# Moving two gate tiles out of the first V buffer, and cutting the last transfers of a cached decode step

## The chip, the cores and the metric

The kernel runs on one core of one Trainium2 chip. The metric is the device time of one execution in microseconds. One execution was also taken by the hardware profiler; its span runs from the first to the last instruction, and its own time is a little longer than that span.

## What is computed

One decode step for two tokens (B = 2, D = 512) with 32 heads of 128 and a cache of 8192 positions per head, all in float32.

```
xn = layernorm(x)
q  = (xn @ wq) as 64 pairs (b, h) of 128
p  = softmax(q . k_cache * 128**-0.5)        # 8192 positions per pair
s  = (p . v_cache) as (2, 4096) @ wo
y  = layernorm(xn)
g  = silu(gelu(y @ w1 + b1) @ w2 + b2)       # F = 1376
out = x + s * g
```

The K cache and the V cache hold 268 MB each. wq and wo are 8.4 MB each, w1 and w2 2.8 MB each. Every byte is read once.

## The kernel before

**Tiles and loop.** The 64 pairs of batch and head are taken two at a time (U = 2): each of N = 32 steps handles 128 partitions by 128 positions by 128 channels, a tile of 8.4 MB for K and one for V. Three buffers of that size exist: `KBUF[0]` and `KBUF[1]` (`big[0]`, `big[1]`) for K, and `VB` (`big[2]`) for V. In step n, DVE multiplies the K tile by the query in place (line 277), reduces it to the scores `SC` (line 278), and takes the row maxima `MX`; PE transposes these, DVE reduces them to `nm`, and PE broadcasts them; ACT turns the scores into the weights `PZ` (line 295) and sums them. PE then multiplies `PZ` with the V tile into the PSUM tile `po` (`weighted`, line 395), ACT copies that to `o4`, and PE folds it into `OT`.

**Order of the work.** There is no planner: `Program.op` writes each instruction to its engine's own queue, with semaphore waits, in the order of the source. Nearly all loads are issued by SP, in source order: the weights, K0 (line 189), K1 (line 266, after the query projection has read wq out of `big[1]`), V0 (line 289), and then in step n the pair K(n+2), V(n+1) (lines 299 and 300). K(n+2) waits for the scores of step n (`k_done`), since it overwrites that buffer; V(n+1) waits for the V product of step n. In step N - 2 the buffer `KBUF[0]` takes the last V tile instead of a K tile (line 302, semaphore `d_v31`), and wo is loaded into `VB` in four pieces along its rows (`WO_CUTS`, lines 303 to 306) once the V product of step N - 2 has read `VB`.

**What the first V buffer holds before V0.** The setup puts small tiles into `big[2]` with `boot` (lines 112 to 122): w1, w2, the layernorm tiles, b2, `q_nat`, `sel`, `z`, `th`, `q_all`. `z` and `th` belong to the gate: ACT copies the second MLP product `pgate` to `z` and takes its tanh into `th` (lines 262 and 263); DVE combines both into `gate` (line 284). That DVE instruction stands in step 0 after the scores of K0. So SP may issue V0 only when `gate` is there:

```
            wait("SP", t["gate"], t["sel"], t["qnat"], pe("pgate"))
            op("SP", "dma_start", VB, vf[0], sig="d_v")
```

**PSUM.** Eight banks are shared between setup and loop. The 64 query rows are spread over partitions by PE into `PB[0]` and `PB[1]` in turn and copied to `Q` by ACT, four steps' worth at a time (line 254). `PB[0]` is bank 0, which later is `po`; `pqa` (the gathered queries) is bank 4, which later is `acc`, the accumulator of the wo product. Both accumulators are zeroed by DVE behind those uses (lines 258 and 259), ahead of the first K multiply in DVE's queue.

**The end.** After the last V product the numerators `OT` and the sums `RS` are rearranged (`Z`, `ZL`, `OA`) and divided (`on`, line 317). The wo product (lines 423 to 428) runs over 32 rows; all rows of a piece wait for that piece's semaphore. DVE multiplies `acc` by the gate, adds x, and two small stores write the result.

Of the kernel before, what the change touches and what calls it, by code (L numbers as in the profile page):

```python
# [13 lines left out]
class Program:  # L14
# [24 lines left out]
    def wait(self, eng, *tokens):  # L39
        for name, v in self.need(eng, tokens):  # L40
            self.engines[eng].wait_ge(self.sem(name), v)
# [5 lines left out]
    def op(self, eng, method, *args, waits=(), sig=None, quiet=False, **kwargs):  # L47
        need = self.need(eng, waits)
        for name, v in need[:-1]:
            self.engines[eng].wait_ge(self.sem(name), v)  # L50
        ins = getattr(self.engines[eng], method)(*args, **kwargs)  # L51
        for name, v in need[-1:]:
            ins._wait_ge(self.sem(name), v)
        if quiet:
            return None
        name = sig or "own_" + eng
        by = 16 if method == "dma_start" else 1
        ins.then_inc(self.sem(name), by)
        self.counts[name] += by
        return name, self.counts[name]  # L60


def decode_kernel(nc, x, kc, vc, wq, wo, w1, b1, w2, b2, out):
    P = 128
# [4 lines left out]
    U = 2  # L69
    HP = P // U  # L70
    KP = S // HP
    HH = H // U
    N = B * HH
# [5 lines left out]
    JW = 512 // DH  # L79
# [4 lines left out]
    OC = DH // PH  # L84
    BH = B * H
    NPB = 512 // DH
    WO_CUTS = (0, 24, 29, 31, 32)

    pr = Program(nc)
    op, wait, take = pr.op, pr.wait, pr.take  # L90

    def sb(shape, name):
        return nc.alloc_sbuf_tensor(name, list(shape), F32).ap()
# [5 lines left out]
    vf = vc.rearrange("b h s d -> (b h s d)").rearrange("(n p j d) -> n p j d", p=P, j=KP, d=DH)  # L99
# [3 lines left out]
    KBUF, VB = rows[:2], rows[2]  # L103
    used = [0]

    def boot(p, n):
        a = used[0]
        used[0] += n
        assert used[0] <= KP * DH
        return big[2][:p, a:a + n]  # L110
# [6 lines left out]
    b2_sb = boot(1, D)  # L117
    q_nat = boot(P, NG // QT * 512).rearrange("p (n c) -> p n c", c=512)
    sel = boot(P, P)
    z = boot(P, P)  # L120
    th = boot(P, P)
    q_all = boot(BH, DH)
    wq_sb = big[1].rearrange("p (c n) -> p c n", n=H * DH)
    wo_sb = big[2].rearrange("p (c n) -> p c n", n=D)
# [1 line left out]
    Q = sb([P, N, DH], "Q")  # L126
# [4 lines left out]
    mod = sb([P, R], "mod")  # L131
# [3 lines left out]
    x4 = sb([P, P], "x4")  # L135
    gate = sb([P, P], "gate")
    res = sb([P, P], "res")
    xnT = sb([P, ND, B], "xnT")
    yT = sb([P, ND, B], "yT")
    hT = sb([P, NF + 1, B], "hT")  # L140
# [13 lines left out]
    on = sb([P, B, OC], "on")  # L154

    bank = [ps([P, 512], f"bank{i}") for i in range(8)]
    po = bank[0]
# [3 lines left out]
    acc = bank[4][:, :P]  # L161
    OA = bank[5][:, :B * (OC + 1)].rearrange("p (b c) -> p b c", c=OC + 1)
    pgate = bank[6][:, :P]
    ph = bank[7][:, :(NF + 1) * B]
    PQ = [bank[1], bank[2]]
    pxn, py = bank[3][:, :ND * B], bank[5][:, :ND * B]
    pqa = bank[4][:, :P]
    PB = [bank[0], bank[7]]

    PE_EVENTS = ["xnT", "yT", "ph", "pq", "pqa"] + [f"pb{g}" for g in range(N // NPB)] + ["pgate"]  # L170

    def pe(name):
        return "pe_setup", PE_EVENTS.index(name) + 1

    def pe_n(name, n):
        return name, n + 1

    t = {}
# [12 lines left out]
    for b in range(B):  # L191
        t["x4"] = op("ACT", "dma_start", x4[b::R, :], x[b, 0].rearrange("(j n) -> j n", n=P), sig="d_x4",
                     waits=[t["x4m"]])
# [11 lines left out]
    for s in range(U):  # L205
        t["half"] = op("DVE", "memset", half[HP * s:HP * (s + 1), PH * s:PH * (s + 1)], 1.0, waits=[a])
    a = op("DVE", "memset", sel, 0.0)
    for k in (1, 2, 6):
        t["mem"] = op("DVE", "memset", bank[k], 0.0)
    by_row = ident.rearrange("p (j r) -> p r j", r=R)  # L210
    t["mod"] = op("DVE", "tensor_reduce", out=mod, in_=by_row, axis=AX.X, op=ALU.add, waits=[t["ident"]])
# [1 line left out]
                  op=ALU.add)  # L213
    t["sel"] = op("DVE", "tensor_copy",
                  sel[:, HP:].rearrange("p (b j r) -> p b j r", b=B, r=HG)[:, :, :QT, 0], by_row[:, :B, :],
                  waits=[a])
# [23 lines left out]
    c = op("DVE", "tensor_mul", gu, gh, gh, waits=[a])  # L240
    c = op("DVE", "tensor_scalar", gu, gu, GELU_A, 1.0, op0=ALU.mult, op1=ALU.add, waits=[c])
    c = op("DVE", "tensor_mul", gu, gu, gh, waits=[c])
    c = op("ACT", "activation", gu, gu, AF.Tanh, scale=GELU_C, waits=[c])
    c = op("DVE", "scalar_tensor_tensor", gu, gu, 1.0, gh, op0=ALU.add, op1=ALU.mult, waits=[c])
    c = op("DVE", "tensor_scalar_mul", hT, gu, 0.5, waits=[c])
# [7 lines left out]
    for g in range(N // NPB):  # L253
        t[f"Q{g}"] = op("ACT", "copy", Q[:, g * NPB:(g + 1) * NPB, :],
                        PB[g % 2].rearrange("p (n d) -> p n d", d=DH), waits=[pe(f"pb{g}")])
        for n in range(g * NPB, (g + 1) * NPB):
            Qt[n] = t[f"Q{g}"]
    t["po0"] = op("DVE", "memset", po, 0.0, waits=[t[f"Q{N // NPB - 2}"]])
    t["acc0"] = op("DVE", "memset", acc, 0.0, waits=[t["qall"]])


    t["z"] = op("ACT", "copy", z, pgate, waits=[pe("pgate")])
# [7 lines left out]
    for n in range(N):  # L270
        k = KBUF[n % U]
        if n:

            op("ACT", "copy", o4, po, sig="s_o4", waits=[pe_n("p_v", n - 1)])
            t["OT"] = op("ACT", "copy", OT[:, U * (n - 1):U * n], pt[:, :U], waits=[pe_n("p_t", n - 1)])
        qb = Q[:, n, :].unsqueeze(1).to_broadcast([P, KP, DH])
        a = op("DVE", "tensor_tensor", out=k, in0=k, in1=qb, op=ALU.mult, waits=[k_land[n], Qt[n]])
        a = op("DVE", "tensor_reduce", out=SC[n % 2], in_=k, axis=AX.X, op=ALU.add, waits=[a], sig="v_k")
        k_done = a
        op("DVE", "tensor_reduce", out=MX, in_=SC[n % 2], axis=AX.X, op=ALU.max, waits=[a], sig="v_mx")  # L280
        op("DVE", "tensor_reduce", out=nm, in_=pm[:1, :P].rearrange("o (s r) -> o s r", s=U), axis=AX.X,
           op=ALU.max, negate=True, waits=[pe_n("p_m", n)], sig="v_nm")
        if n == 0:
            a = op("DVE", "scalar_tensor_tensor", gate, th, 1.0, z, op0=ALU.add, op1=ALU.mult,
                   waits=[t["th"], t["pool"]])
            t["gate"] = a

            wait("SP", t["gate"], t["sel"], t["qnat"], pe("pgate"))
            op("SP", "dma_start", VB, vf[0], sig="d_v")
            t["v_last"] = None  # L290
        a = op("ACT", "copy", bias, pn[:, :1], waits=[pe_n("p_n", n)])
        sc = SC[n % 2].rearrange("p (t j) -> p t j", j=JW)
        for s in range(U):
            r = slice(HP * s, HP * (s + 1))
            op("ACT", "activation", PZ[r, :, s, :], sc[r], AF.Exp, bias=bias[r], scale=SCALE,
               accum_out=RS[r, n:n + 1], waits=[a, t["pool"]], sig="s_pz")
        m = n + 2
        if m < N:
            k_land[m] = op("SP", "dma_start", KBUF[m % U], kf[m], sig=f"d_k{m % U}", waits=[k_done])
            op("SP", "dma_start", VB, vf[m - 1], sig="d_v", waits=[pe_n("p_v", m - 2)])  # L300
        elif m == N:
            op("SP", "dma_start", KBUF[m % U], vf[N - 1], sig="d_v31", waits=[k_done])
            wait("SP", pe_n("p_v", N - 2))
            wo_v = wo.rearrange("(p c) n -> p c n", p=P)
            for i, (c0, c1) in enumerate(zip(WO_CUTS, WO_CUTS[1:])):
                op("SP", "dma_start", wo_sb[:, c0:c1], wo_v[:, c0:c1], sig=f"d_wo{i}")
# [10 lines left out]
    t["on"] = op("DVE", "tensor_tensor", out=on, in0=OA[:, :, :OC], in1=rl.unsqueeze(2).to_broadcast([P, B, OC]),  # L317
                 op=ALU.mult, waits=[a])
    a = op("DVE", "scalar_tensor_tensor", res, acc, 0.5, gate, op0=ALU.mult, op1=ALU.mult,
           waits=[pe_n("p_acc", 0), t["gate"], t["acc0"]])  # L320
    t["res"] = op("DVE", "tensor_add", res, res, x4, waits=[a, t["x4"]])
    for b, eng in enumerate(("SP", "ACT")):
        t[f"o{b}"] = op(eng, "dma_start", out[b, 0].rearrange("(j n) -> j n", n=P), res[b::R, :], sig=f"d_o{b}",
                        waits=[t["res"]])
# [22 lines left out]
    for f in range(NF + 1):  # L347
        for c in range(ND):
            w = w1_sb[:, c, f:NF * P:NF] if f < NF else w1_sb[:, c, F - P:]
            last = f == NF and c == ND - 1  # L350
            mm(ph[:, f * B:(f + 1) * B], w, yT[:, c, :], start=c == 0, stop=c == ND - 1,
               waits=[t["yT"], ("d_w1", 16)], sig="ph" if last else None)
    for n in range(NG // QT):
        for c in range(ND):
            for j in range(QT):
                g = n * QT + j
                last = n == NG // QT - 1 and c == ND - 1 and j == QT - 1
                mm(PQ[n][R * j:R * j + B, :], xnT[:, c, :], wq_sb[:, c, g * 512:(g + 1) * 512], start=c == 0,
                   stop=c == ND - 1, waits=[t["xnT"], t["mem"], ("d_wq", 16)], sig="pq" if last else None)
    for n in range(NG // QT):  # L360
        for hh in range(HG):
            a = HP - (n * QT * HG + hh)
            last = n == NG // QT - 1 and hh == HG - 1
            mm(pqa[:BH, :], sel[:, a:a + BH], q_nat[:, n, hh * DH:(hh + 1) * DH], start=n + hh == 0, stop=last,
               waits=[t["sel"], t["qnat"]], sig="pqa" if last else None)
# [13 lines left out]
    for f in range(NF + 1):  # L379
        for j in range(QT):  # L380
            mm(pgate[R * j:R * j + B, :], hT[:, f, :], w2_sb[:, f, j * P:(j + 1) * P], start=f == 0, stop=False,
               waits=[t["hT"], t["w2"], t["mem"]])
    for j in range(QT):
        mm(pgate[R * j:R * j + B, :], ones[:1, :B], b2_sb[:, j * P:(j + 1) * P], start=False, stop=True,
           waits=[t["b"]], sig="pgate" if j == QT - 1 else None)
# [8 lines left out]

    def weighted(v, last=False):
        take("PE", "s_pz", U)
        if last:
            nc.tensor.wait_ge(pr.sem("d_v31"), 16)
        else:
            take("PE", "d_v", 16)  # L400
        for i in range(NT):
            j = i % QT
            mm(po[R * j:R * j + U * JW, :], PZ[:, i].rearrange("p s j -> p (s j)"),
               v[:, i * JW:(i + 1) * JW, :].rearrange("p j d -> p (j d)"), start=i < QT, stop=i + QT >= NT,
               sig="p_v" if i == NT - 1 else None)
        take("PE", "s_o4")
        for i in range(JW):
            mm(pt[:, :U], o4[:, i * DH:(i + 1) * DH], mod[:, i:U * JW:JW], start=i == 0, stop=i == JW - 1,
               sig="p_t" if i == JW - 1 else None)

    wait("PE", t["po0"], t["pool"], t["mod"])
    softmax()
    with nc.tensor.Fori(0, N - 1):
        weighted(VB)
        softmax()
    weighted(KBUF[0], last=True)

    for b in range(B):
        h = slice(b * H, (b + 1) * H)
        mm(OA[:, b, :OC], Z[:, h].rearrange("p h r -> p (h r)"), mod, waits=[t["Z"]])  # L420
        m = slice(b * HH, (b + 1) * HH)
        mm(OA[:, b, OC:], ZL[:, m].rearrange("p n r -> p (n r)"), ones[:, :1], sig="p_oa" if b == B - 1 else None)
    for i, (c0, c1) in enumerate(zip(WO_CUTS, WO_CUTS[1:])):
        for c in range(c0, c1):
            for j in range(QT):
                last = c == OC - 1 and j == QT - 1
                mm(acc[R * j:R * j + B, :], on[:, :, c], wo_sb[:, c, j * P:(j + 1) * P], start=c == 0,
                   stop=c == OC - 1, waits=[t["on"], t["acc0"], (f"d_wo{i}", 16)], sig="p_acc" if last else None)


_INS = ["A_x", "A_k_cache", "A_v_cache", "A_wq", "A_wo", "B_w1", "B_b1", "B_w2", "B_b2"]
# [23 lines left out]
```

## Time and profile before

| | |
|---|---|
| runs | 1323.99, 1325.63, 1325.75 us, median 1325.63 us |
| profiled execution, its own time | 1324.34 us |
| its span | 1322.9 us |
| DVE busy | 1129.2 us (85%) |
| PE busy | 396.9 us (30%) |
| ACT busy | 70.5 us (5%) |
| read from memory | 559.37 MB, mean 423 GB/s over the span |
| granted TensorE clock, mean | 0.637 |

How to read the profile: times are microseconds from the start of the span. The engines are PE (matmul), PEld (weight load), DVE, ACT, POOL and SP; a trailing q means the queue that issues transfers. A group of instructions is given as line, engine, operation, what it writes and reads by the program's names, shapes, count, busy time and mean duration in ns, and the idle time before it with what ended it. As nearly all instructions are recorded by one helper, they carry that helper's line, L51 (L41 to L50 for its waits), and the names of the tiles tell them apart. A matmul in float32 shows as two records. "GB/s" and "PEclk" give the bytes moved and the granted TensorE clock in equal slices of the span.

### The profile page before, as it was taken

The numbers are of one execution on the slowest core, as the hardware profiler recorded it, in microseconds if no ns is written. First come the engines' busy times: TensorE is split into PE (matmuls) and PEld (weight loads), VectorE is DVE, ScalarE is ACT, GpSimd is POOL, SyncE is SP. The second block draws the span as 40 slices with busy tenths as digits, with TensorE's granted clock in tenths as the row PEclk, the third lists the DMA queues.
The fourth block names the chain that finished last, engine by engine and source line by source line (L and its number), as shares of the span: only waits on it lengthen the run. The fifth ranks groups of instructions, "written<-read, shape, count | busy, mean of one in ns | idle before, by whom it ended". The sixth has DMA issues, their size and how long they took to land. (4 is left out here: it accounts for less than half of the span.)

```text
span 1322.9 us, 7003 instructions
## 1 busy us (share of the span) xinstructions
PE 396.9 (30%) x3128; PEld 144.7 (11%) x3128; DVE 1129.2 (85%) x166; ACT 70.5 (5%) x244; POOL 1.1 (0%) x8
## 2 busy tenths in 40 slices
PE   6603211333231233322123332212333221233336
PEld 6300000000000001000000000000000000000003
DVE  1298988888988888898888889888889988888991
ACT  1100000000000000000000000000000000000000
POOL 0000000000000000000000000000000000000000
PEclk9956656666655666665566666556666655666657
DMA  9939999999999999999999999999999999999997
GB/s 413 427 159 444 432 424 442 430 429 442 430 428 442 430 428 442 434 424 442 438 420 442 438 420 442 440 418 440 442 418 440 442 418 440 442 418 440 442 418 318
DMA packets 10704, 559.51 MB, mean 423 GB/s; under 512 B 1459, under 2 KB 1475, under 8 KB 1862
## 3 DMA queue, kind: packets, MB, share of 16 engines
q1 hardware_dynamic: 10666, 559.36, 97.9%
q8 instruction: 6, 0.10, 0.0%
q14 instruction: 4, 0.03, 0.0%
q10 hardware_dynamic: 28, 0.01, 0.0%
HBM read 559.37 MB, written 0.00 MB: 423 GB/s over the span
## 5 line engine op out<-in xcount | busy, mean ns | idle before, releaser
L51 DVE TENSOR_TENSOR big<-big,Q 128x16384 f32<-128x16384 f32 x32 | 551.2, 17224 | 96.1 <-DMA big<-in_A_k_cache_dram 96.1
L51 DVE TENSOR_REDUCE sc<-big 128x128 f32<-128x16384 f32 x32 | 551.0, 17220 | 1.1
L51 PE MATMUL bank<-big,PZ 128*8 128x512 f32 x2048 | 287.9, 725 | 689.2 <-PEq L45 686.7
L51 PEld LDWEIGHTS bank<-big,PZ 128*8 128x8 f32 x2048 | 59.7, 102 | 890.4 <-issue 887.8
L51 ACT COPY o<-bank 128x512 f32<-128x512 f32 x32 | 18.7, 585 | 939.8 <-PE bank L51 939.8
L51 PE MATMUL bank<-ident,MX 128*1 128x128 f32 x32 | 11.9, 372 | 172.1 <-PEq L45 172.1
L51 PE MATMUL bank<-mod,o 128*128 128x2 f32 x256 | 32.8, 250 | 25.7 <-PEq L45 25.7
L51 PEld LDWEIGHTS bank<-mod,o 128*128 128x128 f32 x256 | 31.0, 191 | 54.4 <-issue 54.4
L51 ACT ACTIVATE PZ<-sc,bias 64x128 f32<-64x128 f32 x64 | 25.5, 399 | 1.9
L51 DVE TENSOR_REDUCE nm<-bank 1x2 f32<-1x128 f32 x32 | 8.9, 279 | 17.8 <-PE bank L51 17.8
L51 DVE MEMSET bank<- 128x512 f32 (+1 forms) x5 | 2.1, 421 | 25.3 <-ACT Q L51 25.1
L51 PEld LDWEIGHTS bank<-ident,MX 128*1 128x1 f32 x32 | 2.5, 79 | 174.1 <-issue 174.1
L51 PE MATMUL bank<-yT,big 128*128 128x2 f32 x88 | 19.9, 364 | 1.9 <-DMA big<-in_B_w_dram 1.9
L51 PEld LDWEIGHTS bank<-yT,big 128*128 128x128 f32 x88 | 19.9, 322 | 2.0 <-DMA big<-in_B_w_dram 2.0
L51 DVE TENSOR_TENSOR gh<-bank,b_sb 128x22 f32<-128x22 f32 x1 | 0.2, 181 | 22.7 <-PE bank L51 22.7
L51 PE MATMUL bank<-nm,srow 1*64 1x1 f32 x128 | 12.0, 243 | 14.8 <-PEq L45 14.8
L51 ACT COPY bias<-bank 128x1 f32<-128x1 f32 x32 | 5.1, 160 | 205.3 <-PE bank L51 205.3
L51 PEld LDWEIGHTS bank<-nm,srow 1*64 1x64 f32 x128 | 10.2, 200 | 24.2 <-issue 24.2
L51 DVE TENSOR_TENSOR Z<-blk,OT 128x256 f32<-128x256 f32 x1 | 0.4, 425 | 14.0 <-ACT OT L51 14.0
L51 ACT ACTIVATION_READ_ACCUMULATOR PZ<-sc,bias 64x1 f32 x64 | 11.8, 185 | 0.0
L51 PE MATMUL bank<-big,xnT 128*2 128x512 f32 x64 | 9.1, 732 | 6.9 <-DMA big<-in_A_wq_dram 6.9
L51 DVE TENSOR_REDUCE MX<-sc 128x1 f32<-128x128 f32 x32 | 9.1, 286 | 1.1
(64 smaller groups left out, 69.4 us busy)
## 6 DMA issues: line engine op xcount, KB each, us to landing
big<-in_A_wo_dram SPq DMA_DIRECT2D x1, 6144.0 KB, 23.7
big<-in_B_w_dram SPq DMA_DIRECT2D x1, 2752.0 KB, 9.4
big<-in_B_w_dram SPq DMA_DIRECT2D x1, 2560.0 KB, 14.9
big<-in_A_wo_dram SPq DMA_DIRECT2D x1, 1280.0 KB, 26.4
big<-in_A_k_cache_dram SPq DMA_DIRECT2D x32, 42.9
big<-in_A_v_cache_dram SPq DMA_DIRECT2D x32, 29.5
big<-in_A_wo_dram SPq DMA_DIRECT2D x1, 512.0 KB, 27.2
big<-in_B_w_dram SPq DMA_DIRECT2D x1, 256.0 KB, 15.3
```

The source lines that it names most:

```text
L51: ins = getattr(self.engines[eng], method)(*args, **kwargs)
```

## The change

- `z` and `th` get tiles of their own in place of parts of `big[2]`. SP's wait ahead of V0 drops `gate`.
- `PB[0]` moves from bank 0 to bank 3 and `pqa` from bank 4 to bank 5. The two later memsets of `po` and `acc` go; banks 4 and 0 are zeroed with banks 1, 2 and 6 at the start, whole.
- The last V tile is loaded in two halves with a semaphore each, and PE waits for a half at a time.
- wo is loaded in seven pieces of 10, 8, 6, 4, 2, 1 and 1 rows in place of 24, 5, 2 and 1.

```diff
-    WO_CUTS = (0, 24, 29, 31, 32)
+    WO_CUTS = (0, 10, 18, 24, 28, 30, 31, 32)
+    V_CUTS = (0, KP // 2, KP)
...
-    z = boot(P, P)
-    th = boot(P, P)
...
+    z = sb([P, P], "z")
+    th = sb([P, P], "th")
...
-    pqa = bank[4][:, :P]
-    PB = [bank[0], bank[7]]
+    pqa = bank[5][:, :P]
+    PB = [bank[3], bank[7]]
...
-    for k in (1, 2, 6):
+    for k in (1, 2, 6, 4, 0):
         t["mem"] = op("DVE", "memset", bank[k], 0.0)
...
-    t["po0"] = op("DVE", "memset", po, 0.0, waits=[t[f"Q{N // NPB - 2}"]])
-    t["acc0"] = op("DVE", "memset", acc, 0.0, waits=[t["qall"]])
...
-            wait("SP", t["gate"], t["sel"], t["qnat"], pe("pgate"))
+            wait("SP", t["sel"], t["qnat"], pe("pgate"))
             op("SP", "dma_start", VB, vf[0], sig="d_v")
-            t["v_last"] = None
...
-            op("SP", "dma_start", KBUF[m % U], vf[N - 1], sig="d_v31", waits=[k_done])
+            for i, (c0, c1) in enumerate(zip(V_CUTS, V_CUTS[1:])):
+                op("SP", "dma_start", KBUF[m % U][:, c0:c1], vf[N - 1][:, c0:c1], sig=f"d_v31{i}", waits=[k_done])
...
-           waits=[pe_n("p_acc", 0), t["gate"], t["acc0"]])
+           waits=[pe_n("p_acc", 0), t["gate"]])
...
-        if last:
-            nc.tensor.wait_ge(pr.sem("d_v31"), 16)
-        else:
+        if not last:
             take("PE", "d_v", 16)
         for i in range(NT):
+            if last and i * JW in V_CUTS:
+                nc.tensor.wait_ge(pr.sem(f"d_v31{V_CUTS.index(i * JW)}"), 16)
...
-    wait("PE", t["po0"], t["pool"], t["mod"])
+    wait("PE", t["mem"], t["pool"], t["mod"])
...
-                   stop=c == OC - 1, waits=[t["on"], t["acc0"], (f"d_wo{i}", 16)], sig="p_acc" if last else None)
+                   stop=c == OC - 1, waits=[t["on"], t["mem"], (f"d_wo{i}", 16)], sig="p_acc" if last else None)
```

## The prediction, made before the result was known

> **What bounds the kernel now.** I read the page first: its slices, queues, groups and transfer list.
>
> ```profile
> GB/s 413 427 159 444 432 424 442 430 429 442 430 428 442 430 428 442 434 424 442 438 420 442 438 420 442 440 418 440 442 418 440 442 418 440 442 418 440 442 418 318
> q1 hardware_dynamic: 10666, 559.36, 97.9%
> L51 DVE TENSOR_TENSOR big<-big,Q 128x16384 f32<-128x16384 f32 x32 | 551.2, 17224 | 96.1 <-DMA big<-in_A_k_cache_dram 96.1
> L51 DVE TENSOR_REDUCE sc<-big 128x128 f32<-128x16384 f32 x32 | 551.0, 17220 | 1.1
> ...
> big<-in_A_wo_dram SPq DMA_DIRECT2D x1, 6144.0 KB, 23.7
> big<-in_A_wo_dram SPq DMA_DIRECT2D x1, 1280.0 KB, 26.4
> big<-in_A_k_cache_dram SPq DMA_DIRECT2D x32, 42.9
> big<-in_A_v_cache_dram SPq DMA_DIRECT2D x32, 29.5
> big<-in_A_wo_dram SPq DMA_DIRECT2D x1, 512.0 KB, 27.2
> big<-in_A_wo_dram SPq DMA_DIRECT2D x1, 256.0 KB, 27.3
> ```
>
> DVE is busiest, but in the loop it waits for K: 96.1 us of idle time before its multiplies ends with a K transfer. The stream from memory runs at 413 to 444 GB/s in every slice but two: the third (159) and the last (318). A K tile takes 42.9 us from issue to landing, more than twice its own transfer (below), so other transfers always lie ahead of it. So the stream sets the pace, and the time is its bytes, plus its pauses, plus what follows its last byte. The change has to be priced on these.
>
> The cadence comes from the timeline of DVE late in the loop, the pause from the windows around the third slice.
>
> ```profile
> 1219.67 17.23 DVE L51 TENSOR_TENSOR big<-big,Q 128x16384 f32<-128x16384 f32 x1 [3.07 <-DMA big<-in_A_k_cache_dram]
> 1258.38 17.23 DVE L51 TENSOR_TENSOR big<-big,Q 128x16384 f32<-128x16384 f32 x1 [3.08 <-DMA big<-in_A_k_cache_dram]
> ...
> 73.00:74.00 1.00, 0.00 (x0) 0.00 (x0) 1.00 (x1) 0.00 (x0) 0.00 (x0) 0.50 0.31 131
> 74.00:93.00 19.00, 0.37 (x1) 0.08 (x1) 18.38 (x4) 0.00 (x0) 0.00 (x0) 0.50 0.00 0
> 93.00:94.00 1.00, 0.38 (x4) 0.32 (x4) 1.00 (x3) 0.21 (x2) 0.00 (x0) 0.50 0.00 0
> 94.00:1296.00 1202.00, 333.90 (x2387) 100.33 (x2387) 1084.53 (x124) 59.39 (x221) 0.00 (x0) 0.62 1.00 433
> ```
>
> One step of K and V takes 1258.38 - 1219.67 = 38.7 us, so one tile 19.35 us. The last column is GB/s: 131 in 73 to 74 is 0.13 MB, 0.3 us at 433 GB/s; then nothing until 94.0. The pause is 73.3 to 94.0, **20.7 us**. From 94 to 1296 there is no other (share 1.00).
>
> What ended it is in the timelines of SP, DVE, PE and the waits of SP's queue:
>
> ```profile
> SPq L51 <- DVE gate L51: 31.9, 1, 31.9
> ...
> 93.36 0.33 SPq L51 DMA_DIRECT2D big<-in_A_v_cache_dram  x1
> 93.74 0.42 SPq L51 DMA_DIRECT2D big<-in_A_k_cache_dram  x1
> 124.69 0.33 SPq L51 DMA_DIRECT2D big<-in_A_v_cache_dram  x1
> 127.75 0.33 SPq L51 DMA_DIRECT2D big<-in_A_k_cache_dram  x1
> ...
> 61.00 0.40 PE L51 MATMUL bank<-big,ones 1*2 1x128 f32 x8
> ...
> 56.98 0.63 DVE L51 MEMSET bank<- 128x512 f32 x2 [25.07 <-ACT Q L51]
> 57.52 17.21 DVE L51 TENSOR_TENSOR big<-big,Q 128x16384 f32<-128x16384 f32 x1
> 74.76 17.22 DVE L51 TENSOR_REDUCE sc<-big 128x128 f32<-128x16384 f32 x1
> 92.01 0.29 DVE L51 TENSOR_REDUCE MX<-sc 128x1 f32<-128x128 f32 x1
> ```
>
> SP sat 31.9 us on `gate`, a small DVE instruction queued behind the 34.4 us of K0's multiply and reduce. `pgate`, the other thing V0 needs, is done at 61.40.
>
> **V0 without the gate.** SP now issues V0 at about 61.5, while K1 is still moving until 73.3. V0 follows it from 73.3 to 92.65. K2 is next. Its wait is for K0's scores: 92.0 as in the trace, or earlier, since K0's multiply was held until 57.52 by the two memsets. Without them it starts when K0 has landed: K0's bytes end one tile before K1's, at 53.95, and a landing comes about 1.4 us behind the last byte (worked out at the tail, below), so at about 55.4, and K2 can be issued at about 89.9. V0 was issued at 93.36 and moved from 94.0, 0.64 us later; even from 92.0 that gives 92.65, no later than V0's end. So K2 follows without a pause, and the stream gains the whole 20.7 us, if no pause comes back. That is checked step by step, with K2 moving 92.65 to 112.0, V1 to 131.35, K3 to 150.7:
>
> ```profile
> 115.38 9.25 PE L51 MATMUL bank<-big,PZ 128*8 128x512 f32 x64 [21.72 <-PEq L45]
> ```
>
> V0 lands at about 94.05; its product takes 9.25 us, so V1 is issued at about 103.5, 8.5 us before its turn (if PE waits for the weights until 94.9, as they follow the gate's row of DVE, still 7.5). K3 waits for K1's scores, at 127.75 in the trace or 2.1 us earlier: 3.6 to 5.7 us before its turn at 131.35. This is the tightest place. From there DVE needs 127.75 - 92.01 = 35.7 us a step against the stream's 38.7, so it gains 3 us a step; in about five steps it waits for K again as it does now, and everything behind lies 20.7 us earlier. DVE's start is thus worth nothing in itself, only margin: the stream hides it.
>
> **Memsets and banks.** The two large memsets added at the start cost what their three neighbours cost, 0.52 us each; they sit ahead of the layernorm on DVE.
>
> ```profile
> 1.72 1.57 DVE L51 MEMSET bank<- 128x512 f32 x3
> 10.22 19.95 PE L51 MATMUL bank<-yT,big 128*128 128x2 f32 x88 [1.95 <-DMA big<-in_B_w_dram]
> ```
>
> PE waits 1.95 us for w1 there, so 1.05 us of delay is hidden; uncovered it would cost at most that on a chain that then waits for wq and K0 anyway. I take 0. The bank moves add no wait, since banks 3 and 5 have been copied out long before; 0.
>
> **The tail.** The order is V30's product, V31's landing, V31's product, `on`, wo's landing, wo's product. From the timelines and windows of the end:
>
> ```profile
> 1289.21 0.43 SPq L51 DMA_DIRECT2D big<-in_A_wo_dram  x1
> ...
> 1295.59 0.18 ACT L51 ACTIVATION_READ_ACCUMULATOR PZ<-sc,bias 64x1 f32 x1
> 1297.09 8.90 PE L51 MATMUL bank<-big,PZ 128*8 128x512 f32 x64 [2.56 <-DMA big<-in_A_v_cache_dram]
> 1309.56 0.36 PE L51 MATMUL bank<-ones,ZL 128*128 128x1 f32 x2
> 1310.16 0.22 DVE L51 TENSOR_TENSOR on<-bank,rl 128x64 f32<-128x64 f32 x1
> 1311.66 8.54 PE L51 MATMUL bank<-big,on 128*2 128x128 f32 x256 [1.74 <-DMA big<-in_A_wo_dram]
> ...
> 1310.00:1311.00 1.00, 0.00 (x0) 0.00 (x0) 0.35 (x2) 0.00 (x0) 0.00 (x0) 1.00 0.97 410
> 1312.00:1313.00 1.00, 1.00 (x28) 0.71 (x20) 0.00 (x0) 0.00 (x0) 0.00 (x0) 0.50 0.94 387
> 1315.00:1316.00 1.00, 1.00 (x48) 0.88 (x40) 0.00 (x0) 0.00 (x0) 0.00 (x0) 1.00 0.16 61
> 1316.00:1317.00 1.00, 1.00 (x48) 0.88 (x40) 0.00 (x0) 0.00 (x0) 0.00 (x0) 1.00 0.01 2
> ```
>
> In the old frame of times: the last wo piece lands at 1289.21 + 27.3 = 1316.5; the last bytes move at about 1315.15 (61 GB/s is 0.06 MB, 0.15 us), which gives the 1.4 us used above. Today PE starts wo at 1311.66, when 24 rows have landed together, and ends at 1320.2, 3.7 us behind the last landing.
>
> V31 in halves: its first half lands 9.7 us before 1297.09, so PE no longer waits for V31 but for the weights, ready at 1295.77. It starts 1.3 us earlier, and its second half is there before PE reaches it. `on`, at 1310.38 today, moves to 1309.1.
>
> wo in seven pieces: a row is 19.35/32 = 0.605 us of the stream, so 10 rows land at 1303.2, 18 at 1308.0, 24 at 1311.7, 28 at 1314.1, and the last at 1316.5. PE starts at 1309.1, 2.5 us earlier. A row is 8 records: 0.17 us at full clock (48 records a us), 0.29 at half (28). At full clock PE catches up with the landings and ends one row behind the last: 1316.8, a gain of 3.4 us. If the clock drops at wo's start, as now, the 8.54 us run from 1309.2 to 1317.7, a gain of 2.5. I take **3.4**: today PE idles from 1309.9 until 1311.66 and the clock is still full in 1310 to 1311; after the change the idle time is only the 0.5 us until `on`. [...]
>
> The three extra wo pieces and the extra half of V cost SP about 0.43 us each, issued while the stream is busy with V31. Whether a piece also costs the stream something: the 512 KB piece landed at 1288.74 + 27.2 = 1315.9 (its issue, from its own row below), the 256 KB piece 0.6 us behind it, which is the 0.6 us of its bytes. So I take 0; the other end is in the first rival.
>
> ```profile
> 1288.74 0.43 SPq L51 DMA_DIRECT2D big<-in_A_wo_dram  x1
> ```
>
> **The sum.** 20.7 + 3.4 = 24.1 us. The profiled execution took 1324.34 us (span 1322.9), which gives 1300.2, span 1298.8. The median of the runs is 1.3 us above that execution, so on its scale **1301.5 us**.
>
> **Rivals.** (1) *Pieces hold the stream.* If each of the four additional transfers kept the stream for the 1.4 us between last byte and landing, the last row would land 5.6 us later, at 1322.1, and PE would end at 1322.3: the tail loses 2.1 us and the time is 1324.34 - 20.7 + 2.1 = 1305.7, or 1307.0 on the median's scale. Against it: the 0.6 us above. 6%. [...]
>
> (2) *The pause comes back.* If DVE ran later under the early V0 by more than the 3.6 us at K3, each further us would reopen the pause; at 5 us of it, 1306.5 on the median's scale. For it: V0 now moves while DVE works on K0. Against: DVE's multiply took 17.21 us while K1 was moving and the reduce 17.22 in the pause. A late K1, sharing the stream with V0, would land by about 94 and cost K3 less than the margin. 4%.
>
> (3) *V0 isn't issued earlier*, held by another of its waits: only the tail remains, 1324.34 - 3.4 = 1320.9, or 1322.2. PE's 61.40 speaks against it. 2%.
>
> (4) *Slower: the stream itself.* Without the pause the stream has some 529 MB (559.4 less the 30.9 of the weights, K0 and K1) to carry at one go. If the rest had kept it fast, it would now run below 433 GB/s. From 433 to 424.6, 2% less, it eats the 24.1 us; at 418, the lowest slice of the page, held throughout, 529 MB take 44 us more, and the time is 1344 (1345.5). Against it: 418 to 442 alternate all through the loop, no slower at its end than behind the pause. 3%.
>
> **How the numbers follow.** The forecast has 85%, the rivals 6, 4, 2 and 3. A measurement of this kernel can tell 0.2%, about 2.7 us, from no change. The forecast and the first two rivals are faster by more; so is most of the third; the fourth is slower: 0.96, 0.01, 0.03. The forecast's own ends are 1301.5 - 1.6 (the lowest run is 1.6 below the median) - about 0.9 for the pause and the landings, 1299.0, and 1301.5 + 0.9 for the half clock, with 1.6 for the runs again, 1304; the range reaches to the first rival, 1307.
>
> **What would show it.** Right: V0's issue at about 61.5; no slice below 400 GB/s but the last; K2's issue at about 90; DVE waiting more than a few us for K only from about K6; V31's product starting with the weights; the wo product in stretches ending within half a us of its last landing; a span near 1299. Wrong: zero GB/s anywhere between 73 and 160, a cadence other than 38.7 us, or a last wo landing more than 2 us behind the last bytes.

## The result, and the profile after

| | before | after |
|---|---|---|
| median of the runs beside each other | 1324.81 us (1323.92 to 1325.75) | 1303.93 us (1301.97 to 1304.48) |
| ratio, 95% interval | | 0.984 (0.9823 to 0.9857) |
| profiled execution, span | 1324.34, 1322.9 us | 1304.39, 1303.1 us |
| start of K31's multiply | 1258.38 us | 1238.27 us |
| from there to the end of the span | 64.5 us | 64.8 us |

The kernel became 20.9 us faster. A second measurement beside the experiments gave 22.0 us (1325.53 to 1303.56). The forecast was 24.1 us less. The last two rows split the difference: the stream came 20.1 us earlier, and the tail gained nothing in this execution.

The changed kernel's slices on the page answer to those of before:

```profile
GB/s 401 444 424 437 429 437 431 433 433 435 433 431 437 433 437 433 435 433 437 428 439 429 439 429 435 433 431 437 431 439 431 437 431 439 429 439 429 439 420 311
```

Its timeline of SP, and then of DVE at K0, K6 and K31:

```profile
61.49 0.33 SPq L51 DMA_DIRECT2D big<-in_A_v_cache_dram  x1
91.27 0.33 SPq L51 DMA_DIRECT2D big<-in_A_k_cache_dram  x1
105.32 0.33 SPq L51 DMA_DIRECT2D big<-in_A_v_cache_dram  x1
127.01 0.33 SPq L51 DMA_DIRECT2D big<-in_A_k_cache_dram  x1
```

```profile
56.77 17.22 DVE L51 TENSOR_TENSOR big<-big,Q 128x16384 f32<-128x16384 f32 x1 [24.93 <-ACT Q L51]
270.56 17.23 DVE L51 TENSOR_TENSOR big<-big,Q 128x16384 f32<-128x16384 f32 x1 [0.26 <-DMA big<-in_A_k_cache_dram]
1238.27 17.23 DVE L51 TENSOR_TENSOR big<-big,Q 128x16384 f32<-128x16384 f32 x1 [3.09 <-DMA big<-in_A_k_cache_dram]
```

The window where nothing moved before (the last column is GB/s):

```profile
74.00:93.00 19.00, 0.74 (x5) 0.40 (x5) 18.39 (x5) 0.04 (x1) 0.00 (x0) 0.50 1.02 442
```

The stream as a whole, in as long a stretch as the prediction took before:

```profile
73.00:1275.00 1202.00, 338.65 (x2392) 101.43 (x2392) 1103.80 (x129) 58.95 (x220) 0.00 (x0) 0.61 1.00 433
```

The slice of 159 GB/s is gone, and where nothing moved, 442 GB/s do; the rate of the stream is 433 GB/s as before. V0 is issued 32 us earlier, K2 at 91.27, K3 at 127.01, all ahead of their turns; DVE first waits for K again at 270.56, which is K6.

The end of the changed kernel, in PE's timeline:

```profile
1275.81 9.96 PE L51 MATMUL bank<-big,PZ 128*8 128x512 f32 x64 [1.38 <-PEq L45]
1288.64 0.64 PE L51 MATMUL bank<-mod,Z 128*128 128x32 f32 x2 [1.04 <-DVE ZL L51]
1291.12 9.21 PE L51 MATMUL bank<-big,on 128*2 128x128 f32 x256 [0.61 <-DVE on L51]
```

In windows of 1 us (the column before the DMA share is the granted clock):

```profile
1288.00:1289.00 1.00, 0.36 (x2) 0.36 (x2) 0.58 (x2) 0.00 (x0) 0.00 (x0) 0.77 0.96 406
1294.00:1295.00 1.00, 1.00 (x28) 0.69 (x20) 0.00 (x0) 0.00 (x0) 0.00 (x0) 0.50 0.66 246
1297.00:1298.00 1.00, 1.00 (x48) 0.90 (x40) 0.00 (x0) 0.00 (x0) 0.00 (x0) 1.00 0.00 0
```

SP's seven issues of wo, and from the page's list the last two pieces with the time from issue to landing:

```profile
1266.57 3.46 SPq L51 DMA_DIRECT2D big<-in_A_wo_dram  x7
```

```profile
big<-in_A_wo_dram SPq DMA_DIRECT2D x2, 256.0 KB, 27.2
```

V31's product no longer waits for V31, and wo's product waits only for `on`. But V31's product took 9.96 us in place of 8.90, and the clock fell to half in 1288 to 1289 (0.77 is full for half of it), ahead of wo's product, which ran until 1300.33. The 27.2 us are the median of the last two pieces (27.0 and 27.4); the very last landed at 1297.0, and PE ended 3.3 us behind it, where the forecast had 0.3.

### The profile page after: what moved, and what is told of

Its sections match the earlier page's. It is cut to its first block, busy times and chain, and to the rows that moved or that the text cites. A ratio compares the mean times of both kernels' runs of the same rounds, so it can differ in the third digit from the quotient of the medians.

```text
span 1303.1 us, 7007 instructions
## 1 busy us (share of the span) xinstructions
PE 404.0 (31%) x3128; PEld 147.0 (11%) x3128; DVE 1129.3 (87%) x166; ACT 70.5 (5%) x244; POOL 1.1 (0%) x8
## 5 line engine op out<-in xcount | busy, mean ns | idle before, releaser
L51 PE MATMUL bank<-big,PZ 128*8 128x512 f32 x2048 | 293.0, 736 | 618.3 <-PEq L45 618.3
L51 PEld LDWEIGHTS bank<-nm,srow 1*64 1x64 f32 x128 | 10.2, 200 | 24.1 <-issue 24.1
L51 PE MATMUL bank<-big,on 128*2 128x128 f32 x256 | 9.2, 317 | 0.6 <-DVE on L51 0.6
(65 smaller groups left out, 65.7 us busy)
```

## The experiments

Theory A: the whole gain is the closed pause of the stream, one for one; the cuts of the tail shorten waits, but PE then starts on a clock at half and gives the time back. The rivals stand in the expectations. The tail below is the time from the start of K31's multiply to the end of the span.

**The gate alone.** z and th in tiles of their own, V0 without the wait for `gate`, all else as before.

```diff
-            wait("SP", t["gate"], t["sel"], t["qnat"], pe("pgate"))
+            wait("SP", t["sel"], t["qnat"], pe("pgate"))
```

> The kernel before with only the gate's part of the change: z and th in tiles of their own, and V0 no longer waiting for gate. Banks, memsets, V31 and wo as before. Theory A (the whole gain is the closed pause, the cuts of the tail gave nothing): the pause in 73 to 94 is gone, K31's multiply starts 20 us earlier than 1258.4, the tail from there to the end keeps its 64.5 us, and the time is 20 to 21 us below the kernel before. Rival B (the pause gave back only some 17 us, and the cuts of the tail gave some 3): 17 us below it.

1304.85 us against 1325.65: ratio 0.9845 (0.9832 to 0.9859), 20.8 us by the medians. DVE's timeline, then PE's:

```profile
1239.17 17.23 DVE L51 TENSOR_TENSOR big<-big,Q 128x16384 f32<-128x16384 f32 x1 [3.07 <-DMA big<-in_A_k_cache_dram]
```

```profile
1277.90 9.66 PE L51 MATMUL bank<-big,PZ 128*8 128x512 f32 x64 [2.58 <-DMA big<-in_A_v_cache_dram]
1292.92 9.07 PE L51 MATMUL bank<-big,on 128*2 128x128 f32 x256 [0.61 <-DVE on L51]
```

K31's multiply is 19.2 us earlier than before and the tail 65.5 us. The tail is 1 us longer than before although nothing in it was changed: V31's product started as long behind K31's multiply as before (38.7 us) and took 9.66 us in place of 8.90. One part of the change holds nearly all of its gain; rival B is out.

**The banks alone.** The two memsets ahead of K0's multiply moved to the start, with the banks that this needs.

> The kernel before with only the PSUM banks moved: the two memsets ahead of K0's multiply gone, two more at the start. Theory A and the prediction: K0's multiply starts up to 2 us earlier, but V0 is still held until the gate, and the stream behind it moves by at most that, since the gate follows K0's scores: a gain of 0.7 to 2 us, all of it a shorter pause. Rival C (the memsets at the start cost what they take, 1 us): no gain or 1 us slower.

1324.75 us, ratio 0.9995 (0.9986 to 1.0004): no difference that can be told. DVE's timeline shows why it was worth less than the 2.1 us of the prediction:

```profile
56.71 17.23 DVE L51 TENSOR_TENSOR big<-big,Q 128x16384 f32<-128x16384 f32 x1 [24.63 <-DMA big<-in_A_k_cache_dram]
```

The multiply starts when K0 lands, at 56.71, not at 55.4; the memsets had held it 0.8 us. V0 was issued 0.8 us earlier (92.57), K31's multiply came at 1257.64, 0.7 us earlier, and the tail was 65.7 us. The time alone does not decide between the 0.7 to 2 us of theory A and the nothing of rival C.

**The tail alone.** V31 in halves and wo in seven pieces, on the kernel before.

> The kernel before with only V31 in halves and wo in seven pieces. Theory A (PE's clock at half takes the gain of the cuts): V31's product starts 1.2 us earlier, at the weights, the wo product starts within 0.6 us of `on`, but both run at half clock for 4 to 6 us, wo's product takes 8.5 to 9.3 us, and the time is within 1.5 us of the kernel before. The prediction's tail: 3.4 us faster. Rival D (each piece holds the stream): the last wo bytes and the last landing come 2 us or more later, and the time is 2 us or more longer.

1324.79 us, ratio 0.9992 (0.9983 to 1.0001), tail 64.7 us. PE's timeline:

```profile
1296.53 9.87 PE L51 MATMUL bank<-big,PZ 128*8 128x512 f32 x64 [1.38 <-PEq L45]
1311.75 9.17 PE L51 MATMUL bank<-big,on 128*2 128x128 f32 x256 [0.61 <-DVE on L51]
```

As theory A has it: both waits are gone and both products are long. The 3.4 us of the prediction are out, and so is rival D as the cause: the last landing came 59.1 us after K31's multiply, against 58.2 before, 0.9 us later and not 2, while PE ended 2.8 us behind it. 0.9 us of gain by the medians lies at the edge of the interval.

**Filling PE's idle time.** The changed kernel with matmuls more in the last step, whose result nobody reads.

```diff
+    def fill(*cols):
+        for c in cols:
+            mm(bank[6][:8, :c], ident[:, :8], Q[:, :JW, :].rearrange("p n d -> p (n d)")[:, :c], waits=[t["z"]])
...
+    weighted(VB)
+    fill(512, 512, 512, 512, 512)
+    softmax()
+    fill(512, 128)
     weighted(KBUF[0], last=True)
...
+    fill(512)
     for b in range(B):
...
+    fill(256)
     for i, (c0, c1) in enumerate(zip(WO_CUTS, WO_CUTS[1:])):
```

A further one of 256 columns stands between V31's product and its fold.

> The changed kernel with 10 matmuls more on PE in the last step, whose result nobody reads: five of 512 columns behind V30's product, 512 and 128 columns behind the last softmax broadcast, 256 columns behind V31's product, 512 ahead of Z's matmuls, 256 ahead of wo's. They fill idle time of PE, so that the clock is full where V31's and wo's products start. Theory A: V31's product takes 7 us in place of 10, wo's product follows the landings and ends within 0.5 us of the last one, and the time is 3 to 4 us below the changed kernel (24 us below the kernel before). Rival E (what the tail waits for is not the clock but the landings or PE's queue): V31's product starts with the weights as before, and the end moves by less than 1 us; with the fillers in the way, up to 1 us later.

1301.91 us, ratio 0.9819 (0.9806 to 0.9833): 23.7 us below the kernel before; its five runs (1301.08 to 1302.57) lie below the changed kernel's median of 1303.56 measured next. PE's timeline, then windows:

```profile
1276.67 7.05 PE L51 MATMUL bank<-big,PZ 128*8 128x512 f32 x64 [0.21 <-PEq L45]
1288.36 6.66 PE L51 MATMUL bank<-big,on 128*2 128x128 f32 x192
1295.28 0.38 PE L51 MATMUL bank<-big,on 128*2 128x128 f32 x2 [0.25 <-DMA big<-in_A_wo_dram]
1296.05 2.14 PE L51 MATMUL bank<-big,on 128*2 128x128 f32 x62 [0.39 <-issue]
```

```profile
1284.00:1286.00 2.00, 1.61 (x11) 1.06 (x10) 0.23 (x1) 0.53 (x2) 0.00 (x0) 1.00 1.00 426
1286.00:1288.00 2.00, 1.91 (x11) 1.17 (x10) 0.71 (x4) 0.00 (x0) 0.00 (x0) 0.85 1.03 436
1288.00:1289.00 1.00, 1.00 (x17) 0.58 (x19) 0.21 (x1) 0.00 (x0) 0.00 (x0) 0.50 0.90 381
```

V31's product takes 7.05 us (granted clock 1.00 from 1276 to 1284), wo's product reaches the landings and waits for them, and the tail is 61.6 us, 2.9 below the kernel before, close to the 61.1 that the prediction implied. The gate alone, measured beside it, took 1304.85 us, so the cuts and the fillers together bring 2.9 us by the medians as well. The last piece landed 58.5 us after K31's multiply, and PE ended 0.4 us behind it in place of 3.3: it is PE that came earlier, not the landings. So most of the gain that was forecast for the tail exists, and the clock had taken it. Rival E is out.

**The changed kernel again**, beside the next three.

> The changed kernel, unchanged, beside the others of this set. All theories: 20 to 22 us below the kernel before; from the start of K31's multiply to the end of the span 64 to 65.5 us, with V31's and wo's products partly at half clock.

1303.56 us, ratio 0.9831 (0.9818 to 0.9844). Here V31's product took 9.07 us and the tail 63.0 us: the last piece landed 58.5 us after K31's multiply, as with the fillers, but PE ended 1.8 us behind it. The clock rose about 4.1 us behind the start of V31's product (0.73 in the window 1280 to 1282, taken as half and then full), against 5.9 us in the first profile of this kernel. So what the cuts bring without fillers differed with where the clock rose and fell in that execution.

**Fillers with the old tail**, V31 whole and wo in four pieces.

> The changed kernel with the fillers, but V31 whole and wo in the old four pieces. Theory A (the cuts and the clock gain only together): `on` comes 3 us earlier, but wo's product waits for its first 24 rows as before, 4 us of idle time in which the clock falls, so it takes 8.5 to 9.5 us from there: within 1 us of the changed kernel without fillers, 2.5 to 3.5 us above the one with fillers and cuts. Rival F (the fillers alone bring the gain, the cuts nothing): within 0.7 us of the one with fillers and cuts.

1306.08 us, ratio 0.9853 (0.9838 to 0.9868): 4.2 us above the kernel with fillers and cuts, and by the ratios no better than the gate alone (0.9845). The profiled execution, the fastest of its runs, had a tail of 64.5 us. Fillers alone bring nothing; rival F is out. PE's timeline:

```profile
1291.24 8.49 PE L51 MATMUL bank<-big,on 128*2 128x128 f32 x256 [2.25 <-DMA big<-in_A_wo_dram]
```

**Fillers in front only** (ahead of V31's product).

> The changed kernel with fillers only ahead of V31's product (behind V30's and behind the last softmax broadcast). Theory A: V31's product takes 7 us and `on` comes some 3 us earlier; wo's product then starts 4 us earlier and has all the time until the last landing even at half clock: within 0.5 us of the kernel with all fillers. If the clock ahead of wo matters as much, 1.5 to 3 us above it.

1301.44 us, ratio 0.9818 (0.9805 to 0.9832), as good as with all fillers. V31's product took 7.05 us; wo's product started at 1287.59 at half clock (0.50 from 1286 to 1292) and still met the landings:

```profile
1287.59 7.87 PE L51 MATMUL bank<-big,on 128*2 128x128 f32 x192 [0.61 <-DVE on L51]
1298.21 0.40 PE L51 MATMUL bank<-big,on 128*2 128x128 f32 x8 [0.23 <-DMA big<-in_A_wo_dram]
```

So a full clock in V31's product was enough: it gave wo's product a start early enough to be slow. In this execution the last piece landed late, 60 us after K31's multiply, and the tail was 63.1 us; PE ended 0.4 us behind the landing.

**Fillers in the middle only** (between V31's and wo's products).

> The changed kernel with fillers only between V31's and wo's products. Theory A, if the fillers hold the clock: V31's product takes 10 us as before, wo's product starts where it did, but runs at full clock for 5.5 us and ends at the last landing: within 0.7 us of the kernel with all fillers, 2 to 3 us below the changed kernel. If they don't hold it (in the kernel with all fillers the clock still fell to 0.50 in 1288 to 1290): no gain, wo's product 9 us.

1303.08 us, ratio 0.9827 (0.9814 to 0.9841), 0.5 us below the changed kernel: neither outcome quite. PE's timeline:

```profile
1275.97 9.61 PE L51 MATMUL bank<-big,PZ 128*8 128x512 f32 x64 [1.38 <-PEq L45]
1290.12 4.55 PE L51 MATMUL bank<-big,on 128*2 128x128 f32 x160
1296.33 2.80 PE L51 MATMUL bank<-big,on 128*2 128x128 f32 x96 [1.66 <-issue]
```

The clock held (1.00 from 1286 to 1299, 160 records in 4.55 us), but PE then stood still for 1.66 us at row 20, with 24 rows landed. The profile names no releaser. One transfer of another queue falls into this time; it began in the window 1293.7 to 1293.9:

```profile
q8 instruction: 1, 0.02, 33.5%
```

These are 16 KB of instructions. By the trace they had moved at 1294.86, and PE went on 1.47 us later. In the profiles before and after PE stands still once each ahead of a matmul for more than 0.3 us with "issue" as the reason, for 1.14 us until 59.60 and for 0.34 us until 59.58, and goes on 1.57 and 1.44 us behind such a transfer (moved at 58.03 and 58.14). What PE waited for in these stops no run tested. As the stop took most of what the fillers could have gained here, and the intervals of the last two kernels overlap (0.9805 to 0.9832 and 0.9814 to 0.9841), it is not shown that fillers in the middle are worth less than those in front.

**Half of V0 early.** The kernel before, V0 in two halves, the first as soon as `pgate` is done, the second behind `gate`.

```diff
-            wait("SP", t["gate"], t["sel"], t["qnat"], pe("pgate"))
-            op("SP", "dma_start", VB, vf[0], sig="d_v")
+            wait("SP", pe("pgate"))
+            op("SP", "dma_start", VB[:, :KP // 2], vf[0][:, :KP // 2], sig="d_v")
+            wait("SP", t["gate"], t["sel"], t["qnat"])
+            op("SP", "dma_start", VB[:, KP // 2:], vf[0][:, KP // 2:], sig="d_v")
```

> The kernel before, with V0 loaded in two halves: the first as soon as pgate is done, the second only after gate, as before; PE waits for both. Theory A (the time follows the pause of the stream one for one): the first half fills 73.3 to 83, 11 us of pause stay, K31's multiply starts near 1248.7 in place of 1258.4, and the time is 9 to 10.5 us below the kernel before. Rival G (the gain comes from something else that V0's early landing frees, PE's first product or SP's queue): with V0 complete no earlier than about 104 and its product no earlier than 105, less than 5 us.

1315.52 us, ratio 0.9925 (0.9912 to 0.9939), 9.9 us of gain by the ratio (0.0075 of 1325.08). Windows, then DVE's timeline:

```profile
83.00:84.00 1.00, 0.00 (x0) 0.00 (x0) 1.00 (x1) 0.00 (x0) 0.00 (x0) 0.50 0.31 131
84.00:93.00 9.00, 0.00 (x0) 0.00 (x0) 9.00 (x1) 0.00 (x0) 0.00 (x0) 0.50 0.03 15
93.00:94.00 1.00, 0.37 (x1) 0.08 (x1) 0.41 (x3) 0.00 (x0) 0.00 (x0) 0.50 0.00 0
94.00:95.00 1.00, 0.38 (x4) 0.32 (x4) 1.00 (x3) 0.16 (x2) 0.00 (x0) 0.50 0.00 0
95.00:96.00 1.00, 0.00 (x0) 0.00 (x0) 1.00 (x1) 0.97 (x4) 0.00 (x0) 0.50 1.50 459
```

```profile
1249.71 17.23 DVE L51 TENSOR_TENSOR big<-big,Q 128x16384 f32<-128x16384 f32 x1 [3.06 <-DMA big<-in_A_k_cache_dram]
```

The pause shrinks to some 11.4 us, from 83.6 to 95 (the 15 GB/s between, 0.13 MB, are 0.3 us of transfer), 9.3 less than before, and K31's multiply moves by 8.7. Time follows the pause one for one, within 1 us. Rival G is out: V0 was not complete before 104, and most of half the gain came all the same.

**Fillers in front, wo in pieces, V31 whole.**

> The changed kernel with the fillers ahead of V31's product, V31 whole, wo in seven pieces. Theory A: V31's product starts at its landing, 1.2 us later than with halves, takes 7 us, and wo's product still has time to catch up with the landings: within 0.7 us of the kernel with fillers in front and both cuts (1301.4). If the halves carry weight once the clock is full, 1 to 1.5 us above it.

1303.07 us, ratio 0.9831 (0.9818 to 0.9845): 1.6 us above the kernel with fillers in front and both cuts by the medians, as in the second outcome. But the two intervals overlap, so the time does not decide what the halves are worth. V31's product started 38.75 us behind K31's multiply (1278.22 and 1239.47), with halves 37.34 (1275.52 and 1238.18): 1.4 us later. wo's product caught up with the landings almost as well: PE ended 0.8 us behind the last one, with both cuts 0.4.

**Fillers in front, V31 in halves, wo in four pieces.**

> The changed kernel with the fillers ahead of V31's product, V31 in halves, wo in the old four pieces. Theory A: wo's product waits for the first 24 rows, idles 4 us or more and runs 8.5 to 9.5 us from there: 2.5 to 4.5 us above the kernel with fillers in front and both cuts, as with the old tail. If the pieces of wo are not what the full clock needs, within 1 us of it.

1305.57 us, ratio 0.985 (0.9835 to 0.9865), 4.1 us above the kernel with fillers in front and both cuts, as theory A has it. PE's timeline:

```profile
1293.01 8.90 PE L51 MATMUL bank<-big,on 128*2 128x128 f32 x256 [5.06 <-DMA big<-in_A_wo_dram]
```

PE waits 5.06 us for the first 24 rows. The clock had fallen ahead of this wait: the four pairs of records of `Z` and `ZL` from 1286.20 on took 0.51 to 0.61 us each, against 0.36 to 0.41 with V31 whole and wo in pieces. So the finer pieces and the full clock go together: each without the other is worth 1 us or nothing. What the halves of V31 add to the two is not settled.

## Why the prediction came out as it did

**The stream's term held.** 20.7 us were forecast, K31's multiply moved by 20.1. Over the nine profiles with an early V0 it started at 1237.99 to 1239.47, over the three with a late one at 1257.64 to 1258.99, so the term is 18.2 to 21.0 us by single executions, and half of V0 gave half of it. That the pause closes without a remainder is shown by the 442 GB/s. What is left of the 20.7 us lies within that scatter and was not settled. The fourth rival, a slower stream, did not show: 433 GB/s before and after. Its price was reckoned from 418 GB/s as the lowest slice of the page; the lowest is 413, the first one, which would have made it some 15 us dearer.

**K0's start was mis-sized and cost nothing.** The step "K0's bytes end one tile before K1's, and a landing comes 1.4 us behind" gave 55.4 us; K0 landed at 56.7. The margin at K3, which was to be 3.6 to 5.7 us, came to 4.3 (131.35 less 127.01), enough. That DVE's start is only margin was right: the banks alone could not be told from no change. The five memsets at the start delayed PE's w1 product by nothing:

```profile
10.16 19.94 PE L51 MATMUL bank<-yT,big 128*128 128x2 f32 x88 [0.82 <-DMA big<-in_B_w_dram]
```

Its wait fell from 1.95 to 0.82 us, the 1.1 us of the memsets, and it still waited for w1.

**The tail's term failed**: 3.4 us forecast, some 1 us measured. Two steps were wrong. First, V31's product was given its old duration with a new start. But its duration was not fixed: it took 7.05 us with the clock full, and half a us more for each us that the clock stayed at half behind its start, 3.8 us of it before (8.90 us), 5.9 us in the changed kernel (9.96 us). In the eight profiles without fillers ahead of it, it took 8.32 to 9.66 us with the old start (four profiles) and 9.07 to 9.96 us with the new one, 1.2 us earlier (four profiles). On the mean it became 0.7 us longer, more than half of what the start gained, and the 8.90 and the 9.96 were each one draw from a scatter of about 1 us.

Second, wo's product was taken at full clock, with half clock as the worse end (2.5 us). It ran about 4.3 us at half (until 1295.4), against 2.9 in the kernel before, and `on` came 0.7 us later than before in the stream's frame (1290.98 + 20.1 against 1310.38), not 1.3 earlier: besides V31's product, the matmuls of Z and ZL ran at half clock as well (1.87 us in place of 1.05, from 1288.64). The rows quoted for "the clock is still full in 1310 to 1311" were read as a property of the idle time; they were a moment in one execution, whose clock fell at 1311.10. The forecast's 48 and 28 records a us count every record that touches a window; by their starts 36 to 40 and 20 began there, so a row took about 0.22 us at full and 0.4 us at half clock, not 0.17 and 0.29.

1303.93 lies at the upper edge of the forecast's own ends, 1304, which allowed 0.9 us for the half clock and 1.6 for the scatter of the runs; the loss in the tail was larger than the one and used up most of the other.

The first rival was not the cause: the pieces cost the stream little, with the last landing 58.7 us after K31's multiply in the changed kernel against 58.2 before.

On the clock: the windows between the times at which it changed in the changed kernel show it whole or half (again the column before the DMA share).

```profile
1281.71:1285.13 3.42, 3.42 (x36) 0.84 (x32) 0.00 (x0) 0.00 (x0) 0.00 (x0) 1.00 1.00 428
1285.13:1288.54 3.41, 1.66 (x16) 0.97 (x8) 0.72 (x2) 0.74 (x2) 0.00 (x0) 1.00 0.99 419
1288.54:1291.95 3.41, 2.70 (x28) 2.40 (x31) 0.44 (x3) 0.00 (x0) 0.00 (x0) 0.50 0.99 412
1291.95:1295.37 3.42, 3.42 (x72) 2.43 (x68) 0.00 (x0) 0.00 (x0) 0.00 (x0) 0.50 0.82 319
```

It fell at 1288.54, after less than 1 us without a matmul but 2.8 us behind the end of V31's product at 1285.77; in between PE only folded and waited. In the profiles before and after every stretch between two changes of the clock is a whole multiple of 3.41 us (6.83, 10.24, 27.31 and 30.72 us through most of the loop). So in these two executions the clock changed on a grid, and the grid lay differently against the work: the clock rose 3.8 us behind the start of V31's product in one and 5.9 us in the other. Records in a stretch did not by themselves hold the clock: with the fillers the profile shows PE busy for 1.61 and 1.91 of 2 us from 1284 to 1288, and the clock fell in that stretch.

What separated the cases was the time of V's products and wo's product alone, without the narrow matmuls of the fold, `Z` and `ZL`. Over the periods of the grid from 95 us to the end of wo's product in these two profiles, a full clock fell at the end of each period with 1.36 us or less of these (64 periods) and held through each with 1.53 us or more (106). A half clock stayed with 2.56 us or less and rose with 2.60 us or more. This is read off the two profiles; no run set out to test it.

## What to carry to other kernels

In a kernel bound by its transfers, look for the time at which nothing moves, and for the small tile that keeps a large buffer from being loaded: two 128 x 128 tiles in the wrong buffer cost 20 us, and moving them gave the pause back one for one. A tail in which PE waits, works briefly and waits again is priced at the clock it will have then, not at the duration it has now, and one profile shows only one draw of it (V31's product took 7.05 to 9.96 us here). Cutting transfers finer paid here only where the work behind them arrived in time and fast enough to follow the pieces: 0.9 us by the medians on the kernel before, at the edge of the interval, and 2.9 us together with the fillers, against the gate alone.

## What the runs showed of the hardware that was not expected

Records that fill PE's time did not always hold the granted clock: with all fillers it fell between 1286 and 1288 at 1.91 of 2 us busy. In the profiles before and after it changed on a grid of 3.41 us and separated by the time of the wide matmuls in a period: a full clock fell after 1.36 us or less of them and held with 1.53 us or more. Pieces of wo of 256 KB landed 0.62 us behind the piece before them in the kernel before, and 0.68 and 0.83 us in the changed kernel; cut into seven, the last landing came 58.5 to 60 us after K31's multiply, 0.3 to 1.8 us later than the 58.2 of the kernel before. PE once stood for 1.66 us in wo's product with its data landed and the clock full, and went on 1.47 us behind a transfer of instructions.
